# Seven block products for gate and val, one PSUM bank for attention

## The chip, the cores and the metric

The kernel runs on one core of a Trainium2 chip. Its time is the device time in microseconds of one execution; the time before is 975.1 us, the median of three runs (974.89 to 975.76). The engines are TensorE (PE, matmuls; its weight loads are listed as PEld), VectorE (DVE), ScalarE (ACT), GpSimd (POOL) and SyncE (SP), which here issues all DMAs, transposing ones too. Every engine works through its own instructions in order; semaphores tie them together.

## The reference

Attention over keys and values that are averaged in groups of eight, then a gated feed-forward layer over all 4608 tokens:

```python
# q, k, v: (8, 8, 576, 64); pool = 8, Sp = 72
k_p = k.reshape(B, H, Sp, pool, D).mean(axis=3)
v_p = v.reshape(B, H, Sp, pool, D).mean(axis=3)
scores = scale * np.matmul(q, k_p.transpose(0, 1, 3, 2))
scores = scores - np.max(scores, axis=-1, keepdims=True)
attn = np.exp(scores)
attn = attn / (np.sum(attn, axis=-1, keepdims=True) + 1e-09)
out = np.matmul(attn, v_p)
...
x = np.ascontiguousarray(attn_out.transpose(0, 2, 1, 3)).reshape(B * S, H * D)
...
g = x @ w_gate                       # (4608, 512) @ (512, 1536)
silu = g * (1.0 / (1.0 + np.exp(-g)))
val = x @ w_val
return (silu * val @ w_out).astype(np.float32)
```

## The kernel before

**Tiles and chunks.** The 4608 tokens go in nine tiles of 512. A tile is worked in twelve chunks of 128 of the 1536 hidden features. `side` makes gate or val of a chunk: x and the weights are kept as a high and a low f16 part, and for each of four blocks of 128 input features it issues three matmuls of 512 token columns (high x high L797, low x high L798, high x low L799), 12 for gate and 12 for val. ACT makes the tanh of gate (L807), DVE `gated` (L810) and `times_val` (L815), which leaves h in val's PSUM bank; ACT copies h to `hh` (fp32r) and `hb` (bf16), and DVE forms the low half `hl` = h - hh (L1080). `project` adds 12 matmuls a chunk (L824, L830, L831) into four accumulator banks, one chunk later than gate and val. `wo_b`, a bf16 copy of w_out, is made by GpSimd in tile 2. After the last chunk `store` copies the accumulators to `ob` and sends them out (L839).

**Banks.** PSUM has eight banks: four accumulators, gv0 and gv1, and two (`ps_att`) in which attention's scores, values and sums take turns.

**Attention.** It goes by pieces of 128 or 64 tokens, five to a tile. `ask` scales and splits the queries (ACT L523 and L524, POOL L525). `front` computes scores of two groups of four heads (PE L542, L543), takes off the maximum (`less_max`, DVE L552 and L553), the exponential (ACT L564), the sums (L571 to L573), splits the weights into `half` (ACT L620 to L625, POOL L630 and L633) and lets SP issue a transposing DMA to `pt` (L637). `back` multiplies by the values (PE L658, L659), divides (DVE L664), makes the high and low part of x (ACT L757, DVE L759) and lets SP transpose them into the tile's x (L764). A tile's gate and val cannot begin before x of all its pieces. `prep` loads and sums k, v and q of the next batch and splits them (POOL L272 to L274, DVE L267, L328, L339 to L360).

**What sets the order.** Tile 0, with the attention of the first two batches, is one hand-written list of jobs (`ORDER`, in `first_tile`). From tile 1 on (`hidden_tiles`), the chunks are the frame, and at four places of each chunk `slot(vector, scalar)` lets the waiting lines of attention go on: back, front, ask and prep are generators that ask for so much DVE and ACT time, and `slot` gives what its room (`ROOM`) allows. If a tile begins and pieces of it are missing, a loop calls `slot` with endless room until they are done. The order on each engine is that in which the program writes its instructions.

## Time and profile before

| | before |
|---|---|
| median of three runs | 975.1 us |
| the profiled execution: span | 973.8 us |
| TensorE busy, granted clock over the span | 97%, 0.993 |
| DVE, ACT, POOL busy | 58%, 47%, 25% |

The span goes from the first to the last instruction of the profiled execution; the runs' times take in what lies around it. Matmul rows overlap one another in the records, so a row's duration is longer than the distance to the next. A row of a group gives the line, engine, operation, what it writes and reads, shapes and count, then busy us and mean ns of one, then the engine's idle time ahead of these instructions and what ended it. A row of what an engine waits for gives us in total, times, and the longest. A row of the timeline gives start and duration in us.

### The profile page before, as it was taken

The numbers are of one execution on the slowest core, as the hardware profiler recorded it, in microseconds if no ns is written. First come the engines' busy times: TensorE is split into PE (matmuls) and PEld (weight loads), VectorE is DVE, ScalarE is ACT, GpSimd is POOL, SyncE is SP. The second block draws the span as 40 slices with busy tenths as digits, with TensorE's granted clock in tenths as the row PEclk, the third lists the DMA queues.
The fourth block names the chain that finished last, engine by engine and source line by source line (L and its number), as shares of the span: only waits on it lengthen the run. The fifth ranks groups of instructions, "written<-read, shape, count | busy, mean of one in ns | idle before, by whom it ended". The sixth has DMA issues, their size and how long they took to land.

```text
span 973.8 us, 14306 instructions
## 1 busy us (share of the span) xinstructions
PE 939.7 (97%) x5486; PEld 498.4 (51%) x5486; DVE 566.0 (58%) x1005; ACT 461.2 (47%) x864; POOL 241.3 (25%) x327
## 2 busy tenths in 40 slices
PE   5779999799999999999999999999999999999998
PEld 4657545354555555554555555554545555444443
DVE  6788877667766675586446675674444454323222
ACT  3898883245554553544254544552454443222222
POOL 4533336035226230521025211620121201000000
PEclk9899999999999999999999999999999999999999
DMA  9855426246437342653047232840231222001001
GB/s 349 237 154 208 154 109 171 80 115 186 92 109 211 102 83 79 187 127 82 13 88 235 57 70 87 251 86 15 77 83 43 71 66 55 11 1 44 0 1 44
DMA packets 155524, 103.02 MB, mean 106 GB/s; under 512 B 113216, under 2 KB 141888, under 8 KB 153920
## 3 DMA queue, kind: packets, MB, share of 16 engines
q1 hardware_dynamic: 155456, 102.11, 37.3%
q8 instruction: 43, 0.70, 0.3%
q14 instruction: 25, 0.20, 0.1%
HBM read 67.63 MB, written 9.44 MB: 79 GB/s over the span
## 4 chain that ended last, share of the span: by engine, by line
PE 87%; DMA 6%; POOL 2%; ACT 2%; issue 1%; DVE 1%; SPq 0%; POOLq 0%; DVEq 0%; ACTq 0%
PE gv L797 18%; PE gv L798 18%; PE gv L799 18%; PE acc L824 10%; PE acc L830 9%; PE acc L831 9%; DMA pt<-half 2%; DMA kr<-k_rows 1%; DMA in<-v_rest 1%; DMA in<-k_rows 1%; PE ps L542 1%; PE ps L658 1%; PE ps L543 1%; PE ps L659 1%; DMA k<-k_rows 1%
## 5 line engine op out<-in xcount | busy, mean ns | idle before, releaser
L797 PE MATMUL gv<-x,wgv_h 128*128 128x512 f16 (+1 forms) x888 | 332.0, 374 | 3.8 <-ACT x L669 1.8
L798 PE MATMUL gv<-x,wgv_h 128*128 128x512 f16 (+1 forms) x888 | 331.8, 374 | 1.3 <-DVE x L673 1.3
L799 PE MATMUL gv<-x,wgv_l 128*128 128x512 f16 (+1 forms) x888 | 331.9, 374 | 0.5 <-DVE wgv_l L253 0.5
L810 DVE SCALAR_TENSOR_TENSOR hf<-hf,gv 128x512 f32<-128x512 f32 (+1 forms) x111 | 74.1, 668 | 171.6 <-ACT hf L807 171.3
L807 ACT ACTIVATE hf<-gv,un 128x512 f32<-128x512 f32 (+1 forms) x111 | 74.8, 674 | 193.9 <-PE gv L799 193.9
L1076 ACT CAST hh<-gv 128x512 fp32r<-128x512 f32 x96 | 56.3, 586 | 227.2 <-DVE gv L815 227.2
L831 PE MATMUL acc<-hb,wo_l 128*128 128x512 bf16 x384 | 145.5, 379 | 0.0
L824 PE MATMUL acc<-hh,wo_h 128*128 128x512 f32 (+1 forms) x444 | 139.5, 436 | 0.0
L799 PEld LDWEIGHTS <-wgv_l 128*128 128x128 f16 x888 | 87.0, 98 | 102.2 <-issue 1.7
L798 PEld LDWEIGHTS <-wgv_h 128*128 128x128 f16 x888 | 87.0, 98 | 98.1 <-issue 4.7
L797 PEld LDWEIGHTS <-wgv_h 128*128 128x128 f16 x888 | 87.4, 98 | 94.3
L1080 DVE TENSOR_TENSOR hl<-gv,hh 128x512 bf16<-128x512 f32 x96 | 66.3, 691 | 111.0 <-ACT hb L1077 111.0
L525 POOL TENSOR_TENSOR box<-qt,box 64x512 f16<-64x512 f32 (+1 forms) x60 | 64.0, 1067 | 227.8 <-issue 160.9
L815 DVE SCALAR_TENSOR_TENSOR gv<-gv,un,hf 128x512 f32<-128x512 f32 (+1 forms) x111 | 82.3, 741 | 63.0 <-PE gv L799 62.3
L830 PE MATMUL acc<-hl,wo_b 128*128 128x512 bf16 x288 | 109.8, 381 | 0.0
L824 PEld LDWEIGHTS acc<-hh,wo_h 128*128 128x128 f32 x444 | 83.2, 191 | 24.2 <-ACT hh L969 0.3
L630 POOL TENSOR_TENSOR half<-sc,half 128x512 f16<-128x512 f32 (+1 forms) x30 | 34.7, 1158 | 215.8 <-ACT half L620 193.6
L831 PEld LDWEIGHTS <-wo_l 128*128 128x128 bf16 x444 | 43.7, 98 | 37.9
L1077 ACT CAST hb<-gv 128x512 bf16<-128x512 f32 x96 | 56.8, 591 | 0.0
L830 PE MATMUL acc<-hl,wo_h 128*128 128x512 bf16 (+1 forms) x156 | 56.7, 368 | 0.0
L830 PEld LDWEIGHTS <-wo_b 128*128 128x128 bf16 x288 | 28.3, 98 | 42.2 <-issue 16.6
L523 ACT ACTIVATE qt<-qt,inv 128x512 f32<-128x512 f32 (+1 forms) x60 | 40.9, 682 | 0.0
(143 smaller groups left out, 1121.5 us busy)
## 6 DMA issues: line engine op xcount, KB each, us to landing
ws<-w_all SPq DMA_DIRECT2D x12, 1536.0 KB, 7.1
qt<-q_twice SPq DMA_DIRECT2D x48, 256.0 KB, 3.2
out_t<-ob SPq DMA_DIRECT2D x36, 256.0 KB, 2.3
in<-k_rows SPq DMA_DIRECT2D x12, 576.0 KB, 3.9
in<-q_rows SPq DMA_DIRECT2D x12, 576.0 KB, 5.2
in<-v_main SPq DMA_DIRECT2D x12, 512.0 KB, 4.3
in<-v_rest SPq DMA_DIRECT2D x12, 512.0 KB, 5.7
qt<-q_rows SPq DMA_DIRECT2D x8, 256.0 KB, 4.3
```

Source lines behind the costliest of these rows:

```text
L525: nc.gpsimd.tensor_sub(o[rows], qt[rows], o[rows])
L797: nc.tensor.matmul(o, wh, x["h"][:, j, a:e], start=(j == 0), stop=False)
L798: nc.tensor.matmul(o, wh, x["l"][:, j, a:e], start=False, stop=False)
L799: nc.tensor.matmul(o, wl, x["h"][:, j, a:e], start=False, stop=(j == NJ - 1))
L807: nc.scalar.activation(hf, gate, AF.Tanh, scale=un[:, c, 0:1])
L810: nc.vector.scalar_tensor_tensor(out=hf, in0=hf, scalar=1.0, in1=gate, op0=ALU.add, op1=ALU.mult)
L815: nc.vector.scalar_tensor_tensor(out=out, in0=val, scalar=un[:, c, 2:3], in1=hf, op0=ALU.mult, op1=ALU.mult)
L824: nc.tensor.matmul(o, wo_h[:, c, js], hh[:, :n], start=begin, stop=False)
L830: nc.tensor.matmul(o, wo[:, c, js], hl[:, :n], start=False, stop=False)
L831: nc.tensor.matmul(o, wo_l[:, c, js], hb[:, :n], start=False, stop=end)
L1077: nc.scalar.copy(hb[:, :n], val)
L1080: nc.vector.tensor_sub(hl[:, :n], val, hh[:, :n].bitcast(F32))
```

## The change

**Seven products.** From tile 2 on, nine of the twelve chunks (0 to 8; chunks 9 to 11 come first in the tile, as before) get gate and val by Strassen's scheme in Winograd's form. The 2 x 2 blocks of the weights are gate and val by the first and second half of the input features; those of x are feature halves by halves of the 512 tokens. Each of seven products is six matmuls of 256 columns (`product`, L997). The sums of products are made in PSUM by accumulation, by two ACT copies of 128x256 (one within a bank, one into the gate bank), an ACT copy to SBUF (`rs`) and two DVE additions of 128x256 (L1284, L1331). A chunk's products 5, 1, 6 and 2 are issued during the chunk ahead of it. Val turns between the banks gv1 and gv2.

**Sums of weights and of x.** In tile 1, `fast_weights` makes for each of the nine chunks the four weight sums: one DVE addition of the high and low parts (L940, into the single buffer `fw`), four on GpSimd (L942 to L945), ACT copies to f16, and three on GpSimd for the low halves (L958). `fast_x` does the like for x at the start of each tile from 2 on (L965, L967 to L970, L975), in two halves. Both are a new line, `extra`, that `slot` serves first.

**Attention.** From chunk 8 of tile 1 on, scores, values and sums share one bank, and the two groups of scores go one after the other. `front` is cut in two (`front`, `soft`), k's and q's sums are made in halves, and the planner keeps a running time of PE, DVE and ACT (`now`) from which the room of each slot is worked out. The numbers `LANDS` and `CLEAR` keep a sum away from its load, and a bank away from its reader.

**The rest.** h is written to SBUF by `times_val`; its low half is made by GpSimd in the nine chunks, by DVE in the others (L1258); `hb` and `wo_b` become strided views of hh and of w_out. k's sums and the values of the first batches share memory with `xc`.

The core of the diff:

```diff
-ROOM = (1200, 1200), (1200, 1500), (1200, 1200), (2400, 1200)
+ROOM = (2500, 2500)
+FAST = 9
+FAST_ROOM = (3400, 2800), (2700, 2100), (1400, 900), (0, 0), (2000, 0), (2000, 1900), (2400, 4200)
+FAST_FIRST, FAST_THEN = 3, 5
+ONE_BANK = (1, 8)
 LEAD = 3
-AHEAD = 3
+LANDS = 3800
+CLEAR = 650
+AHEAD = 9
...
-    ps_att = ctx.enter_context(tc.tile_pool(name="ps_att", bufs=2, space=bass.MemoryType.PSUM))
+    early = ctx.enter_context(tc.tile_pool(name="early", bufs=1))
+    ps_att = ctx.enter_context(tc.tile_pool(name="ps_att", bufs=1, space=bass.MemoryType.PSUM))
...
-        pss = scores(b, s0, m, t["qs"])
...
+        for groups in ((0,), (1,)) if now["one"] else ((0, 1),):
+            pss = scores(b, s0, m, t["qs"], groups=groups)
...
+    def fast_weights(c):
+
+        yield 1400, 0
+        f = xp.tile([P, 2 * DM], F32, name="fw", tag="f", bufs=1)
+        g_h, g_l = (a[:, c].rearrange("p i j f -> p (i j f)") for a in (wgv_h, wgv_l))
+        nc.vector.tensor_add(f, g_h, g_l)
+        a11, a12, a21, a22 = (f[:, i * HT : (i + 1) * HT] for i in range(4))
+        nc.gpsimd.tensor_add(a22, a21, a22)
+        nc.gpsimd.tensor_sub(a21, a11, a21)
+        nc.gpsimd.tensor_sub(a11, a22, a11)
+        nc.gpsimd.tensor_sub(a12, a12, a11)
+        yield from after(3500)
+        yield 0, 1300
...
+        for o, cs in outs[:2]:
+            nc.scalar.copy(o, f[:, cs])
+        for (o, cs), (hi, _) in zip(outs[2:], outs[:2]):
+            for at in range(cs.start, cs.stop, TILE):
...
+                nc.gpsimd.tensor_sub(o[:, w], f[:, at:e], hi[:, w])
...
+    def product(o, k, c, x, xc, begin):
+
+        for j in range(HJ):
...
+            for n, (a, b) in enumerate(((w[0], xh), (w[0], xl), (w[1], xh))):
+                nc.tensor.matmul(
+                    o, a, b, start=begin and j + n == 0, stop=j == HJ - 1 and n == 2,
+                    skip_group_check=True,
+                )
...
+                    def fourth():
+                        slot(*FAST_ROOM[4])
+                        if new:
+                            seed_fast(new)
+                        slot(*FAST_ROOM[5])
+                        product(t["r"], 4, c, x, xc, False)
+                        times_val(hf, hf, t["val"], un, c)
+                        hh = high_of(hf, n)
+                        slot(*FAST_ROOM[6])
+                        pending.append((acc, *ends, i, c, hh, low_of(nc.gpsimd, hf, hh, n)))
```

**A chunk on DVE.** This is DVE's row in a chunk of tile 3 with attention beside it, before: `gated`, attention's low part of x, `times_val` and the low half, then two operations of `prep`.

```order
L810 SCALAR_TENSOR_TENSOR hf<-hf,gv_3321 128x512
L759 SCALAR_TENSOR_TENSOR box<-ps,r,box 128x512
L815 SCALAR_TENSOR_TENSOR gv_3322<-gv_3322,un,hf 128x512
L1080 TENSOR_TENSOR hl<-gv_3322,hh 128x512
L477 TENSOR_TENSOR mx_3197<-mx_3197 128x1
L328 TENSOR_REDUCE mx_3197<-box 128x1 x2
```

The same place of a chunk with seven products, after (`rs` is the kept product, L734 attention's division, L845 its low part of x):

```order
L901 SCALAR_TENSOR_TENSOR hf<-hf,gv_4867 128x512
L1331 TENSOR_TENSOR gv_4822<-gv_4822,rs 128x256
L734 TENSOR_TENSOR ps<-ps,ri 128x512
L907 SCALAR_TENSOR_TENSOR hf<-gv_4822,un,hf 128x512
L845 SCALAR_TENSOR_TENSOR box<-ps,r,box 128x512
L1284 TENSOR_TENSOR gv_4974<-gv_4918,rs 128x256
```

The low half has left DVE and two additions of half the width have come in, one of them for the chunk that follows.

**Tile 1 on GpSimd and DVE.** Before, GpSimd has query splits (L525), batch sums (L272 to L274) and the low half of attention's weights there:

```order
L525 TENSOR_TENSOR box<-qt,box 64x4x128 x4
L272 TENSOR_TENSOR in<-in 128x2x256
L273 TENSOR_TENSOR in<-in 128x2x128
L274 TENSOR_TENSOR box<-in 128x128
L272 TENSOR_TENSOR in<-in 128x2x256
L273 TENSOR_TENSOR in<-in 128x2x128
L274 TENSOR_TENSOR box<-in 128x128
```

After, GpSimd from the last sum of one weight build to the low halves that free its buffer (L587 is the query split, L283 to L285 the batch sums, L671 and L672 the low half of attention's weights):

```order
L945 TENSOR_TENSOR fw<-fw 128x256
L587 TENSOR_TENSOR box<-qt,box 64x4x128
L283 TENSOR_TENSOR in<-in 128x2x256
L284 TENSOR_TENSOR in<-in 128x2x128
L285 TENSOR_TENSOR box<-in 128x128
L283 TENSOR_TENSOR in<-in 128x2x256
L284 TENSOR_TENSOR in<-in 128x2x128
L285 TENSOR_TENSOR box<-in 128x128
L671 TENSOR_TENSOR half_130<-sc,half_130 128x512
L672 TENSOR_TENSOR half_130<-sc,half_130 128x2x32
L958 TENSOR_TENSOR ws_l<-fw,ws_h 128x512
L958 TENSOR_TENSOR ws_l<-fw,ws_h 128x256
```

And DVE in tile 1, after, where L940 fills `fw` for the next build:

```order
L901 SCALAR_TENSOR_TENSOR hf<-hf,gv_2099 128x512
L940 TENSOR_TENSOR fw<-wgv_h,wgv_l 128x1024
L907 SCALAR_TENSOR_TENSOR hf<-gv_2100,un,hf 128x512
L1258 TENSOR_TENSOR hl<-hf,hh 128x512
L614 TENSOR_REDUCE mx<-ps 128x4
L615 TENSOR_TENSOR sc<-ps,mx 128x288
L614 TENSOR_REDUCE mx<-ps 128x4
L615 TENSOR_TENSOR sc<-ps,mx 128x288
```

On GpSimd ten other operations stand inside a build, and on DVE the fill of `fw` stands ahead of `times_val`, the low half and `less_max`.

**The start of tile 3.** SP before, at the last transpose into tile 3's x (`x_2888`), followed by transposes of attention's weights and queries for the pieces behind, and only then tile 2's output:

```order
L764 DMA_TRANSPOSE x_2888<-box_1705 128x8x64
L637 DMA_TRANSPOSE pt_3742<-half0_132 128x16x128
L509 DMA qt_3788<-q_twice 128x4x128
L509 DMA qt_3790<-q_twice 128x4x128
L637 DMA_TRANSPOSE pt_3874<-half1_133 128x16x128
L839 DMA out_t<-ob_3984 128x512 x2
```

SP after, the same place (`x_2986` is tile 3's x, `x_4133` tile 4's):

```order
L850 DMA_TRANSPOSE x_2986<-box_1470 128x8x128
L557 DMA qt_4088<-q_twice 128x4x128
L557 DMA qt_4090<-q_twice 128x4x128
L707 DMA_TRANSPOSE pt_4122<-half0_129 128x16x128
L850 DMA_TRANSPOSE x_2986<-box_1702 128x8x64
L850 DMA_TRANSPOSE x_4133<-box_1470 128x8x128
L1009 DMA out_t<-ob_4238 128x512 x2
```

And DVE after, between the last `times_val` of tile 2 and the first use of tile 3's x (L614 and L615 are `less_max`, L632 to L638 sums of attention):

```order
L907 SCALAR_TENSOR_TENSOR hf<-gv_3904,un,hf 128x512
L845 SCALAR_TENSOR_TENSOR box<-ps,r,box 128x512
L632 TENSOR_REDUCE sm<-sc 64x8
L637 TENSOR_SCALAR sm<-sm 64x8
L638 RECIPROCAL ri<-sm 64x8
L614 TENSOR_REDUCE mx<-ps 128x4
L615 TENSOR_TENSOR sc<-ps,mx 128x288
L614 TENSOR_REDUCE mx<-ps 128x4
L615 TENSOR_TENSOR sc<-ps,mx 128x288
L734 TENSOR_TENSOR ps<-ps,ri 64x512
L632 TENSOR_REDUCE sm<-sc 128x8
```

Two score groups and the values of tile 3's last piece now stand between the two tiles, and the transpose into x_2986 comes right ahead of tile 2's output and behind pt_4122, which belongs to a later piece.

## The prediction

> **What bounds the kernel now.** I read the page's totals and chain first, then the busy time by stretches, then what TensorE (PE) waits for, then single rows.

> ```profile
> PE 939.7 (97%) x5486; PEld 498.4 (51%) x5486; DVE 566.0 (58%) x1005; ACT 461.2 (47%) x864; POOL 241.3 (25%) x327
> ...
> PE 87%; DMA 6%; POOL 2%; ACT 2%; issue 1%; DVE 1%; SPq 0%; POOLq 0%; DVEq 0%; ACTq 0%
> PE gv L797 18%; PE gv L798 18%; PE gv L799 18%; PE acc L824 10%; PE acc L830 9%; PE acc L831 9%; DMA pt<-half 2%; DMA kr<-k_rows 1%; DMA in<-v_rest 1%; DMA in<-k_rows 1%; PE ps L542 1%; PE ps L658 1%; PE ps L543 1%; PE ps L659 1%; DMA k<-k_rows 1%
> ```

> The chain of waits is PE for 87%, and 54% of it is the three gate/val lines. The stretches (busy us of PE, PEld, DVE, ACT, POOL, then granted clock, DMA share, GB/s) say where that holds:

> ```profile
> 150.00:240.00 90.00, 83.82 (x499) 43.50 (x496) 61.88 (x103) 35.61 (x68) 32.58 (x41) 1.00 0.52 145
> 600.00:690.00 90.00, 90.00 (x513) 45.74 (x512) 53.89 (x98) 38.90 (x78) 22.89 (x30) 1.00 0.42 113
> 780.00:870.00 90.00, 90.00 (x484) 45.07 (x482) 35.42 (x58) 29.98 (x57) 5.45 (x8) 1.00 0.14 36
> ```

> In the tiles that the change rewrites, PE is never idle, while DVE has 36 us of 90 free beside full attention, ACT 51 and POOL 67. So PE time that goes comes off the end, until something else is late. All that PE waits for is short:

> ```profile
> PE ps L536 <- DVE ksum L267: 8.5, 2, 6.9
> PE ps L646 <- DMA pt<-half: 4.1, 3, 2.7
> PE ps L381 <- DMA vr<-v_main: 2.5, 2, 1.4
> PE ps L181 <- DVE sc L553: 2.4, 1, 2.4
> ```

> **What PE gains.** PE rows overlap, so the price of a matmul is the distance of starts. First the gate and val sides of a chunk in the last tile, with the matmul ahead of them (start, duration), then a 256-column side in tile 0, and the group of weight loads (busy time, mean ns):

> ```profile
> 856.47 0.38 PE L831 MATMUL acc<-hb,wo_l 128*128 128x512 bf16 x1
> 856.69 0.38 PE L797 MATMUL gv<-x,wgv_h 128*128 128x512 f16 x1
> ...
> 861.65 0.38 PE L799 MATMUL gv<-x,wgv_l 128*128 128x512 f16 x1
> ```

> ```profile
> 85.99 0.28 PE L797 MATMUL gv<-x,wgv_h 128*128 128x256 f16 x1
> ...
> 87.20 0.27 PE L799 MATMUL gv<-x,wgv_l 128*128 128x256 f16 x1
> ...
> L797 PEld LDWEIGHTS <-wgv_h 128*128 128x128 f16 x888 | 87.4, 98 | 94.3
> ```

> 24 matmuls (gate 12, val 12) start within 4.96 us: 4.96 / 23 = 0.2157 us each. Twelve of 256 columns start within 1.21 us: 1.21 / 11 = 0.110, which I carry as 0.109, as half the columns would have it. So half the columns cost half the time although each loads its own weights; the loads' 98 ns stay below it. A projection matmul takes 0.22 (856.47 to 856.69), and a chunk 5.18 + 12 x 0.22 = 7.8. A changed chunk issues 7 products x 6 = 42 x 0.109 = 4.58 us for 24 x 0.2157 = 5.18: 0.595 less. Nine chunks in seven tiles are 63: **37.5 us off PE**. Projection keeps its twelve matmuls. Replacing the copy of w_out by a strided view costs nothing: both forms stand in before.

> ```profile
> L830 PE MATMUL acc<-hl,wo_b 128*128 128x512 bf16 x288 | 109.8, 381 | 0.0
> L830 PE MATMUL acc<-hl,wo_h 128*128 128x512 bf16 x132 | 50.3, 381 | 0.0
> ```

> **What is added on the other engines.** A changed chunk adds two DVE sums of 128x256 and two ACT copies of 128x256 (estimates of 0.43 and 0.4, from the 128x288 row L553 below and half of L620), drops ACT's hb cast, and sends DVE's low half to GpSimd. Prices (busy time, mean ns | idle before):

> ```profile
> L630 POOL TENSOR_TENSOR half<-sc,half 128x512 f16<-128x512 f32 x24 | 27.8, 1159 | 160.1 <-ACT half L620 138.0 <-DVE sm L571 11.9 <-ACT half L621 10.3
> L272 POOL TENSOR_TENSOR in<-in 128x512 f32<-128x512 f32 x24 | 30.6, 1273 | 14.4 <-DMA in<-v_main 7.9 <-issue 2.2 <-DVE sm L571 2.0
> L273 POOL TENSOR_TENSOR in<-in 128x256 f32<-128x256 f32 x24 | 17.8, 743 | 1.9
> L274 POOL TENSOR_TENSOR box<-in 128x128 f32<-128x128 f32 x24 | 11.3, 470 | 1.9
> L525 POOL TENSOR_TENSOR box<-qt,box 64x512 f16<-64x512 f32 x48 | 55.8, 1163 | 174.8 <-issue 114.2 <-PE ps L543 30.3 <-ACT box L524 28.4
> L1080 DVE TENSOR_TENSOR hl<-gv,hh 128x512 bf16<-128x512 f32 x96 | 66.3, 691 | 111.0 <-ACT hb L1077 111.0
> ```

> The low half takes 1.16 there for 0.69. It is wanted by the fifth matmul of the chunk's projection, behind 3 us of other products, so in steady chunks PE covers it. Walked through one chunk by these prices, each DVE or ACT result that the seven products need is ready 0.8 to 3 us of PE work ahead; I take nothing there, with 0 to 3 us over all for the range. If that cover were gone, 0.5 us a chunk would be 31 us, most of the gain. The x sums at each start of a tile take two halves of a DVE sum (1.38), four 128x256 on GpSimd (3.0), an ACT cast (1.2) and two 128x512 on GpSimd (2.3): 16 us, and up to 23 with attention's work between, in the 21.7 us that three normal chunks leave. That is 0 to 1.5 us a tile; I take 2 in sum. The tail has the last low half on GpSimd, 0.5 longer; with its hand-over I take 1.

> **Tile 1.** Nine weight builds stand in it. One issues on GpSimd four 128x256 (4 x 0.743), one 128x512 (1.16) and two 128x256 of low halves: 5.6 us, nine 50.5. Beside them stand four batch sums (1.273 + 0.743 + 0.470 = 2.49 each, 9.9), nine query splits (1.163, 10.5) and the low halves of attention (6.6): 78 us in the 86 that eleven chunks of 7.8 us leave. There is one `fw` buffer, so L940 of the next build waits on DVE for GpSimd's last L958, with times_val (L907), the low half (L1258) and less_max (L614, L615) queued behind it, and PE behind those. If GpSimd never starves, PE loses 2.4 to 4 us; walking the order by these durations I get 5.1 and 2.5 us before two value groups and 6.3 and 2.3 before two score groups, 16 together. Builds can slide against the waits of others, which the walk doesn't let them; I take 7, nearer the low end, and keep both ends.

> **Starts of tiles.** A tile's first matmul needs x of all its pieces. At tile 3's start the order puts two score groups on the one bank and then the values of the last piece with no chunk between, and SP has the transpose of another piece's weights ahead of x's. Prices of that chain:

> ```profile
> L552 DVE TENSOR_REDUCE mx<-ps 128x4 f32<-128x288 f32 x64 | 28.8, 450 | 4.7 <-PE ps L536 2.5 <-PE ps L543 2.1
> L553 DVE TENSOR_TENSOR sc<-ps,mx 128x288 f32<-128x288 f32 x64 | 29.3, 458 | 4.0
> L564 ACT ACTIVATE sc<-sc,logunit,p2s 128x576 f32<-128x576 f32 x24 | 21.0, 876 | 8.1 <-DVE sc L553 8.1
> L620 ACT CAST half<-sc 128x512 f16<-128x512 f32 x24 | 14.7, 612 | 0.2
> L664 DVE TENSOR_TENSOR ps<-ps,ri 128x512 f32<-128x512 f32 x24 | 16.6, 690 | 0.0
> L757 ACT ACTIVATE box<-ps,r 128x512 f16<-128x512 f32 x24 | 16.7, 694 | 18.5 <-DVE ps L664 17.1 <-issue 1.4
> L759 DVE SCALAR_TENSOR_TENSOR box<-ps,r,box 128x512 f16<-128x512 f32 x24 | 17.8, 743 | 0.8 <-ACT box L757 0.8
> ```

> ```profile
> pt<-half SPq DMA_TRANSPOSE x40, 3.7
> x<-box SPq DMA_TRANSPOSE x30, 2.8
> L637 SPq DMA_TRANSPOSE pt<-half x40: 1225/1592/3304, 26.9 to 823.3; - x40
> ```

> There the chain is 2 x (0.3 scores + 0.91 max and difference) = 2.4, exp 0.88, casts 2.1 (L620 and the smaller ones), the rest of the weights' low half on GpSimd 0.5, issue of pt 1.6, landing of x 2.8: 10.3 us, in which PE has little to do: 10. At tile 2's start PE has 2.6 us of projection after the last val side; behind that side stand on DVE L907 (0.76), the cast (0.6), L1258 (0.69) and L845 (0.74), then x's landing (2.8): 5.6 us, so 3 stay open, and up to 6 with pt's issue in front. I take 5. At tile 5's start L845 stands behind the last L907: 0.76 + 0.74 + 2.8 = 4.3 with 1.3 of PE work: 3. The other tiles have x earlier. Sum **18**; if pt's transpose is through early 10, with every chain 2 us longer 24.

> **One bank.** From tile 1's chunk 8 the two score groups go one after the other, which is in these walks; 2.4 us of old waiting at one bank (L181 above) go.

> **The sum** against the profiled 973.8: -37.5, +7 (tile 1), +18 (starts), +2 (x sums), +1 (tail), -2.4 = 961.9. The median of the three runs, 975.1, stands 1.3 over the span: **963 us**.

> **A clock.** In 40 to 80 us, where PE was idle for 8.8 of 40 us, the granted clock fell to 0.87:

> ```profile
> 40.00:80.00 40.00, 31.18 (x241) 23.99 (x241) 30.68 (x58) 35.34 (x56) 13.17 (x18) 0.87 0.68 184
> ```

> So three long stalls may cost a microsecond or two each besides; 0 to 5 is in the range and not in the sum. [...]

> **Rivals.** *A, all is covered.* Builds slide, starts lose 3 to 6 us only: 973.8 - 37.5 + 3 + 5 + 1 + 1.3 = 946 to 950. For it: DVE, ACT and POOL have room in every stretch. Against: the order at tile 3's start has no PE work to cover the chain.

> *B, DVE and GpSimd block one another in tile 1, and it ends slower.* Rows of before show an operation standing while the other engine has one under way:

> ```profile
> 102.20 1.85 DVE L210 TENSOR_SCALAR ws<-ws 128x1536 uint16<-128x1536 uint16 x1
> 102.43 2.54 POOL L587 TENSOR_TENSOR sc<-sc,ri 128x576 f32<-128x576 f32 x1 [3.36 <-DVE ri L583]
> ...
> 120.68 1.15 POOL L587 TENSOR_TENSOR sc<-sc,ri 128x576 f32<-128x576 f32 x1 [3.33 <-DVE ri L583]
> L253 DVE SCALAR_TENSOR_TENSOR wgv_l<-wf,sw,wgv_h x24: 732/746/1757, 47.8 to 154.5; 128x512 f16<-128x512 f32 x24
> ```

> L587 took 2.54 beside L210 and 1.15 alone. L940 reads two SBUF tensors (estimate 2 x 0.69 = 1.38), and the low half of normal chunks now reads SBUF twice as well. Nine and twelve of them are 12.4 + 8.3 = 20.7 us in which GpSimd would stand; its 78 become 99 in 86, 13 over, and with the walk's 16 tile 1 costs up to 29: 963 - 7 + 16 to 29 = 972 to 985. It decides from 17 us in tile 1. [...]

> *C, the seven products cost more than 0.109 each*, by alternating x and sums or because weight loads of 98 ns leave 11 ns only: at 0.112, 63 x 42 x 0.003 = 8 us more, 971. Against it: the 256-column side is exactly such a row of loads.

> *D, the steady chunks are not covered*: 31 us as above, 994. Against it: the free time of DVE and ACT in those stretches.

> **How the numbers follow.** Forecast, by the bounds of tile 1 and the starts 951 to 972, 0.50; A 0.18; B 0.20; C 0.08; D 0.04. The range takes most of A and nearly all of B: **944 to 984**. About 0.2% (2 us) is what a measurement tells from no change. Faster than 973 are the forecast, A and most of C, 0.73; within 0.2% the upper edges of the forecast and C and the lower of B, 0.05; slower the rest of B, and D, 0.22.

> **What would show it.** 256-column rows 0.109 apart in tiles 2 to 8 with no idle of PE inside them prove the gain. The waits of PE should name L940 or L907 or less_max in 130 to 215 (7 us; over 16 is B, with L942 to L958 longer than 0.75 and 1.2), and x's transposes at the starts of tiles 2, 3 and 5 (5, 10, 3). The forecast is wrong if PE waits inside steady chunks, or if the starts show no idle.

## The result and the profile after

| | before | after |
|---|---|---|
| median | 975.4 us (4 runs) | 1029.0 us (4 runs, 1023.2 to 1033.3) |
| ratio after / before | | 1.054 [1.049, 1.058] |
| profiled span | 973.8 us | 1030.5 us |
| mean granted clock of TensorE | 0.993 | 0.967 |

The change makes the kernel 5.4% slower; the prediction was 963 us, 944 to 984. From the page of after, the totals, the granted clock in tenths over 40 slices, and the chain by engine:

```profile
PE 929.0 (90%) x6521; PEld 610.2 (59%) x6620; DVE 616.6 (60%) x1115; ACT 502.2 (49%) x989; POOL 444.8 (43%) x525
...
PEclk9889999988989999799999899999999999999999
...
PE 60%; DVE 14%; POOL 10%; DMA 6%; issue 5%; ACT 5%; SPq 1%; POOLq 0%; DVEq 0%; ACTq 0%
```

PE's share of the chain fell from 87% to 60%; DVE and POOL together went from 3% to 24%. PE's busy time fell by only 10.7 us, since rows at a lower clock are longer (after 200 us L883's of 512 columns take 0.63 us at clock 0.50 and 0.38 at 1.00, medians; e5 below, the same matmuls at a clock of 1.00 from 188 to 969 us, has 911.3). GpSimd is 43% busy over the span, yet its part of the chain went from 2% to 10%: an average does not show where it is full. The stretches of tiles 1 to 4 and of tile 7 do (columns as in the prediction); below them stand tiles 1 and 2 of before:

```profile
188.00:318.00 130.00, 109.29 (x581) 53.63 (x591) 76.24 (x124) 53.54 (x107) 86.64 (x105) 0.91 0.35 87
318.00:434.00 116.00, 100.98 (x747) 68.16 (x758) 78.73 (x151) 54.95 (x114) 51.89 (x61) 0.93 0.39 102
434.00:542.00 108.00, 97.20 (x748) 66.20 (x759) 67.86 (x125) 54.51 (x121) 52.37 (x61) 0.98 0.44 112
542.00:655.00 113.00, 100.05 (x735) 67.16 (x744) 69.32 (x130) 53.67 (x115) 53.09 (x61) 0.97 0.40 102
...
854.00:946.00 92.00, 90.50 (x627) 61.86 (x636) 35.01 (x61) 31.04 (x64) 22.32 (x23) 1.00 0.15 27
...
```

```profile
188.00:290.00 102.00, 101.02 (x601) 51.83 (x598) 70.82 (x135) 51.41 (x105) 31.96 (x40) 1.00 0.44 117
290.00:390.00 100.00, 100.00 (x610) 51.25 (x609) 63.93 (x114) 48.22 (x99) 35.18 (x51) 1.00 0.45 119
```

In these two tiles of before PE idled 1.0 us; in the four of after it idles 20.7, 15.0, 10.8 and 13.0, at a granted clock of 0.91 to 0.98. Tile 7, with attention only up to 871 us, is hardly ever idle. What PE waits for, after (the largest first, without one row of tile 0):

```profile
PE ps L604 <- DVE box L845: 11.6, 11, 3.1
PE ps L728 <- DMA pt<-half: 8.8, 2, 6.5
...
PE ps L604 <- DVE sc L615: 7.6, 8, 2.0
PE ps L728 <- DVE box L845: 6.5, 5, 2.2
PE ps L604 <- POOL box L587: 6.2, 3, 4.1
PE ps L604 <- DVE x L743: 5.7, 1, 5.7
```

All are attention's score and value groups (L604, L728). Those for L845 and L615 are at the bank, which DVE has yet to read; the others are for GpSimd's split of the queries, for a transfer, and in tile 1, where attention still had two banks, for L743. The products' own waits (L997) stand further down, 7.3 us together.

**Theories.** *S*: the sums cost the time, as *W* those of the weights, as *X* those of x. As *G* they do it by GpSimd's time, as *Q* because what follows in DVE's and ACT's queues stands behind them; as *F* the fill of the single buffer `fw` (L940) is what holds DVE. *B*: the one bank costs it. *P*: the planner's new order costs it. *L*: the seven products themselves do not gain.

### The profile page after: what moved, and what is told of

It is laid out like the page before. It is cut to its first block, busy times and chain, and to the rows that moved or that the text cites. A ratio compares the mean times of both kernels' runs of the same rounds, so it can differ in the third digit from the quotient of the medians.

```text
span 1030.5 us, 16984 instructions
## 1 busy us (share of the span) xinstructions
PE 929.0 (90%) x6521; PEld 610.2 (59%) x6620; DVE 616.6 (60%) x1115; ACT 502.2 (49%) x989; POOL 444.8 (43%) x525
## 3 DMA queue, kind: packets, MB, share of 16 engines
q1 hardware_dynamic: 155456, 102.11, 37.5%
## 4 chain that ended last, share of the span: by engine, by line
PE 60%; DVE 14%; POOL 10%; DMA 6%; issue 5%; ACT 5%; SPq 1%; POOLq 0%; DVEq 0%; ACTq 0%
PE gv L997 24%; PE acc L919 18%; PE gv L883 5%; PE gv L884 4%; PE gv L885 4%; DMA pt<-half 2%; DVE hf L907 2%; POOL box L587 2%; DMA in<-q_rows 1%; POOL xc L975 1%; DVE hf L901 1%; PE ps L398 1%; DVE fx L965 1%; PE ps L604 1%; POOL ws_l L958 1%
## 5 line engine op out<-in xcount | busy, mean ns | idle before, releaser
L1258 POOL TENSOR_TENSOR hl<-hf,hh 128x512 bf16<-128x512 f32 x63 | 81.5, 1293 | 195.4 <-ACT hh L1252 193.3
L919 PE MATMUL acc<-hl,wo_h 128*128 128x512 bf16 (+1 forms) x413 | 154.8, 377 | 4.6 <-POOL hl L1258 0.2
L883 PE MATMUL gv<-x,wgv_h 128*128 128x512 f16 (+1 forms) x384 | 145.5, 379 | 11.2 <-DMA x<-box 4.2
L884 PE MATMUL gv<-x,wgv_h 128*128 128x512 f16 (+1 forms) x384 | 145.2, 378 | 1.3 <-DVE x L743 1.3
L885 PE MATMUL gv<-x,wgv_l 128*128 128x512 f16 (+1 forms) x384 | 145.3, 378 | 0.8 <-DVE wgv_l L264 0.8
L919 PE MATMUL acc<-hh,wo_l 128*128 128x512 bf16 (+1 forms) x376 | 143.7, 385 | 2.4 <-issue 0.6
L587 POOL TENSOR_TENSOR box<-qt,box 64x512 f16<-64x512 f32 (+1 forms) x60 | 66.5, 1109 | 140.8 <-ACT box L586 113.6
L997 PEld LDWEIGHTS <-wgv_h 128*128 128x128 f16 x1008 | 98.3, 98 | 42.2 <-issue 6.3
L907 DVE SCALAR_TENSOR_TENSOR hf<-gv,un,hf 128x512 f32<-128x512 f32 x96 | 71.8, 748 | 59.8 <-PE gv L997 37.9
L997 PE MATMUL gv<-xc,wgv_h 128*128 128x256 f16 x504 | 90.0, 274 | 5.1 <-DVE gv L1331 4.1
L997 PE MATMUL gv<-xc,ws_h 128*128 128x256 f16 x504 | 89.9, 274 | 2.6 <-ACT gv L1278 2.6
L997 PE MATMUL gv<-x,wgv_h 128*128 128x256 f16 x504 | 91.3, 277 | 0.0
L997 PEld LDWEIGHTS <-ws_h 128*128 128x128 f16 x756 | 73.0, 98 | 27.6 <-issue 4.2
L1284 DVE TENSOR_TENSOR gv<-gv,rs 128x256 f32<-128x256 f32 x63 | 27.2, 432 | 72.0 <-PE gv L997 60.4
L997 PE MATMUL gv<-x,wgv_l 128*128 128x256 f16 x252 | 69.7, 276 | 0.0
L997 PE MATMUL gv<-xc,ws_l 128*128 128x256 f16 x252 | 69.1, 274 | 0.0
```

The source lines that it names most:

```text
L587: nc.gpsimd.tensor_sub(o[rows], qt[rows], o[rows])
L883: nc.tensor.matmul(o, wh, x["h"][:, j, a:e], start=(j == 0), stop=False)
L884: nc.tensor.matmul(o, wh, x["l"][:, j, a:e], start=False, stop=False)
L885: nc.tensor.matmul(o, wl, x["h"][:, j, a:e], start=False, stop=(j == NJ - 1))
L907: nc.vector.scalar_tensor_tensor(out=out, in0=val, scalar=un[:, c, 2:3], in1=hf, op0=ALU.mult, op1=ALU.mult)
L919: nc.tensor.matmul(acc[j][:, a:e], w[:, c, j * P : (j + 1) * P], h[:, :n], start=begin and at < NJ, stop=end and w is wo_l,)
```

## The experiments

Every time is a median of 4 to 12 runs beside runs of before on the same chip. For most kernels I also read the length of each tile, from the first projection matmul of a tile to that of the next (of tile 8 to that of its last chunk):

| us, tile | 1 | 2 | 3 | 4 | 5 | 6 | 7 | 8 |
|---|---|---|---|---|---|---|---|---|
| before | 101.5 | 100.8 | 99.3 | 100.6 | 98.5 | 100.1 | 96.2 | 81.2 |
| after | 131.3 | 116.1 | 107.8 | 113.1 | 98.5 | 100.0 | 91.6 | 77.1 |
| e1, no products, no sums | 105.8 | 105.9 | 104.2 | 108.3 | 104.1 | 106.2 | 97.0 | 81.5 |
| e2, as e1 with two banks | 102.9 | 104.1 | 103.7 | 100.5 | 99.0 | 100.6 | 96.2 | 81.5 |
| e5, products, no sums | 105.8 | 99.6 | 101.3 | 103.2 | 100.5 | 100.8 | 92.8 | 77.1 |
| e4, no builds | 106.9 | 102.2 | 108.9 | 107.0 | 109.6 | 100.0 | 91.8 | 77.1 |
| e6, no x sums | 131.1 | 109.9 | 102.3 | 102.9 | 100.8 | 100.8 | 92.7 | 77.1 |
| e20, sums without GpSimd | 111.2 | 110.0 | 101.7 | 108.3 | 98.0 | 99.4 | 91.7 | 77.0 |
| e9, later fill of fw | 114.9 | 143.3 | 102.5 | 111.8 | 98.9 | 100.0 | 91.7 | 77.1 |

Tile 1 of after, which has the builds, is 30 us longer than before; tiles 7 and 8 together are 8.7 us shorter, and tiles 5 and 6 the same.

### Taking the change apart

**e1_no_products**: no chunk by seven products, no sums; planner, one bank and hh view stay.

```diff
-FAST = 9
+FAST = 0
```

> The seven products and all their sums are gone (twelve normal chunks in every tile); the one attention bank from tile 1's chunk 8, the halved score groups and the new planner stay. PE's work is that of before. If the sums of weights and x on GpSimd and DVE made the loss (theory S), the waits go with them: 973 to 980, and no half clock after 100 us. If the one bank made it (theory B), the waits of the scores and values for L845 and L615 (27 us in the changed kernel) stay, with some of the half clock: 995 to 1015.

Measured 1009.6 against 976.7, ratio 1.034 [1.032, 1.035]. A good half of the loss is there without one product or sum. The waits of PE in e1:

```profile
PE ps L604 <- DVE sc L615: 10.6, 13, 1.2
...
PE ps L728 <- DVE box L845: 7.9, 10, 1.3
```

23 short stalls, 18.5 us: a score group waits until `less_max` has read the group ahead of it out of the bank, a value group behind the same DVE queue.

**e2_no_products_two_banks**: the same with attention on two banks.

```diff
-ONE_BANK = (1, 8)
+ONE_BANK = (99, 0)
```

> As the run without products, and attention keeps two banks to the end (val stays in one bank); both score groups go together again. Only the new planner, the low half of h from SBUF and the strided views are left of the change. S and B: 970 to 978. If the planner's own order is bad (theory P: attention too late), 985 or more, and PE waits for x at the starts of tiles.

Measured 984.3, 1.008 [1.007, 1.010]. So the one bank costs 25 us (1009.6 - 984.3) and what is left of the change 8 (984.3 - 976.7).

**e5_no_sums**: products stay, neither sums of weights nor of x; the products read unsummed parts.

```diff
-                join("extra", fast_x(x, xc))
...
-                        join("extra", fast_weights(c))
```

> The whole change, but no sums of weights and of x are made; the products take parts of the weights and of x themselves (same matmuls, wrong output). One bank stays. S: tile 1 falls back by 20 to 25 us, the starts of tiles by 2 to 5 us each: 960 to 985. B: only tile 1's 17 us of builds and some x sums go, the waits for the bank stay in tiles 2 to 4: 1000 to 1010.

Measured 977.8, 1.001 [0.999, 1.003], as S has it. Against e1 the seven products take off 32 us; L falls. What the products gain pays for the one bank and the planner's order and nothing more, and adding the sums costs all the rest, 51 us (1029.0 - 977.8).

**e3_two_banks**: products and sums stay, attention gets its second bank from an accumulator (the fourth block of the projection is added to the third).

```diff
+                if (i, c) == ONE_BANK:
+                    free_banks[:] = [(ps_att, "att"), (ps_acc, "acc3")]
```

> The whole change, but attention has two banks: the fourth output block of the projection is added into the third's accumulators from tile 1 on (same matmuls, the output of these two blocks is wrong), and its bank goes to attention. B: the waits for L845 and L615 fall from 27 to under 8 us and half of the half clock in tiles 2 to 4 goes: 985 to 1000. S: little of it, 1012 to 1030, with tile 1 still 20 us longer than before.

Measured 1036.3, 1.062 [1.059, 1.065]: slower than after, where B had to gain. Waits of PE in e3:

```profile
PE ps L604 <- DVE box L845: 18.0, 8, 5.5
...
PE gv L998 <- POOL xc L976: 11.2, 2, 8.7
...
PE gv L998 <- ACT xc L974: 6.4, 2, 4.3
```

The waits at the bank did not go, and waits of the first products for the x sums (L974, L976, the casts and low halves of xc) came beside them. So the bank's 25 us are its price where no sums stand beside it; with the sums a second bank alone gives nothing back. With it the score groups also go together again and the planner no longer keeps `CLEAR`; why it is worse stays open.

**e4_no_weight_sums** and **e6_no_x_sums**: one of the two sums left out, and the products that would read them read unsummed parts.

```diff
-                    if i == 1 and c < FAST:
-                        join("extra", fast_weights(c))
```

> The whole change without the weight builds of tile 1 (products 3, 6 and 7 take unsummed weights, wrong output); x sums stay. Without both it was 977.8, with both 1029.0. If the builds carry the loss, also that of tiles 2 to 4 by what they push behind (theory W): 980 to 990, tile 1 under 108 us. If the x sums at the tile starts carry that of tiles 2 to 4 (theory X): 1000 to 1010, only tile 1 shorter.

```diff
-                join("extra", fast_x(x, xc))
```

> The whole change without the sums of x (products take x itself, wrong output), with the weight builds. The x sums cost 20 us where no builds stood. If the two add up: 1006 to 1012. If x sums only cost because attention is behind by then: under 1000 or over 1015.

Measured 998.3, 1.022 [1.018, 1.025], and 1014.4, 1.039 [1.037, 1.041]. The builds cost 31 us beside x sums (1029.0 - 998.3) and 37 without (1014.4 - 977.8), the x sums 15 and 20. Tile 1 alone falls from 131.3 to 106.9 without builds. Neither run lies in a range expected: e4 is between W and X, and e6 2 us above what adding up would give.

**e20_sums_without_gpsimd**: DVE's and ACT's part of both sums stays, GpSimd's operations in them go.

```diff
-        nc.gpsimd.tensor_add(a22, a21, a22)
...
-            nc.gpsimd.tensor_sub(b11, b12, b11)
```

> The whole change, with the sums' DVE additions and ACT casts, but without their GpSimd operations (the four sums and the low halves of weights and of x; wrong output). Without any sums it was 977.8, with all 1029.0. If GpSimd's time is what the sums cost (theory G): 978 to 990. If it is the DVE and ACT work standing in their queues (theory Q): 1000 to 1025.

Measured 994.6, 1.019 [1.017, 1.020]. It lies between G and Q. Of the sums' 51 us, 34 go with GpSimd's part (1029.0 - 994.6) and 17 stay with the rest, so G takes some two thirds and Q one third; but what DVE and ACT lose by waiting for GpSimd's results goes here with G.

**e7_low_half_dve**: the low half of h goes back from GpSimd to DVE in the 63 chunks.

```diff
-                        pending.append((acc, *ends, i, c, hh, low_of(nc.gpsimd, hf, hh, n)))
+                        pending.append((acc, *ends, i, c, hh, low_of(nc.vector, hf, hh, n)))
```

> The whole change, but the low half of h stays on DVE in the nine chunks too. In tiles 2 to 8 GpSimd loses 63 x 1.29 us of work and DVE gains 63 x 0.69. If GpSimd's load in steady tiles is a part of the loss (theory G): 1010 to 1020. If DVE, which reads the one bank, is what is short there (theory B): 1030 to 1045. Tile 1 stays at 131 us in both.

Measured 1094.8, 1.122 [1.118, 1.126]. Sixty-three operations of 0.69 us (43 us, L1080 of before) on an engine that is 60% busy cost 66 us, far beyond both expectations; the planner's rooms were left as they are. Waits of PE in e7:

```profile
PE ps L604 <- DVE sc L615: 20.6, 15, 5.1
PE ps L728 <- DVE box L845: 15.7, 6, 5.1
PE gv L883 <- DMA x<-box: 15.4, 5, 4.1
```

The same waits as in after, the first two 2.4 to 2.7 times as long: DVE's queue sets when the bank comes free and when x is there. That part of the change helps.

### Giving the waits room

**e8_no_products_clear**: e1, with the planner keeping 2000 ns between a bank and its reader.

```diff
-CLEAR = 650
+CLEAR = 2000
```

> The run without products on one bank, with CLEAR 2000 for 650: the planner leaves 2 us of PE work for 0.65 between a reader of the bank and the next writer. If the one bank costs because the next score or value group comes before DVE has read the bank (theory B): the 22 us of waits for L615 and L845 fall under 6, 984 to 992. If it costs because attention as a whole gets too late or by PE work in between: 1005 or more.

Measured 991.3, 1.015 [1.012, 1.018]: 18 us less than e1, and the waits for L615 and L845 are gone from the top. In their place, in e8:

```profile
PE ps L728 <- DMA pt<-half: 9.4, 4, 3.4
```

So most of B's price without sums is the planner's distance, not the bank as such; some of it turns into later attention weights. The whole change with this distance alone was not run.

**e9_late_fill**: a build waits 3.5 us more before it is done, so that the next L940 finds `fw` free.

```diff
+        yield from after(3500)
```

> The whole change, but the next weight build is asked for only 3.5 us of PE work after the last low half of the one ahead. If tile 1 is long because L940 stands on DVE waiting for the single buffer (12 us of DVE idle there, with times_val and less_max behind it; theory F): these waits go, tile 1 falls by 10 to 15 us, 1010 to 1020, also if two builds slip into tile 2. If GpSimd's work itself is what attention waits for (theory G): tile 1 falls by under 6 us and what is gained comes back in tile 2, 1022 to 1035.

Measured 1035.2, 1.059 [1.056, 1.062]. Tile 1 falls by 16 us, and DVE's waits at L940 from 12.4 to 0.6, as F has it; tile 2 rises by 27, with the last two of the nine builds now in front of its x sums in the same line. The first wait of PE in e9:

```profile
PE gv L998 <- ACT xc L974: 25.7, 2, 19.6
```

So the wait for the single buffer was a cause of tile 1's length, but not of the whole loss: the amount of work stays, and two builds moved into tile 2 cost more there than the wait did.

**e10_spread_clear**: three chunks by products in tile 2, six in tile 3, nine from tile 4; builds in tiles 1 to 3; CLEAR 2000.

```diff
+FAST_IN = {1: 0, 2: 3, 3: 6}
```

> Correct variant: builds spread over tiles 1 to 3 (three each; tile 2 has three chunks with products, tile 3 six, from tile 4 nine), and CLEAR 2000. Nine of the 63 chunks lose 0.56 us each, 5 us. If W and B hold, both costs shrink: 955 to 975. If not, 990 or more.

Measured 999.5, 1.023 [1.019, 1.026]. It is the second branch expected. Tiles 1 to 4 are 39 us longer than before, tiles 5 to 8 together 13 shorter.

**e11_two_banks_wait**: e2 with later use of what attention makes.

```diff
-LEAD = 3
+LEAD = 4
...
-WAIT = 3
+WAIT = 5
```

> The run without products on two banks, with WAIT 5 for 3 and LEAD 4 for 3: a piece's values come two slots later. If the 8 us that this planner costs over before are values ahead of their transposed weights (PE waits for pt 4 us), 974 to 979; if they are attention's order as such, 982 to 988.

Measured 986.1, 1.009 [1.007, 1.012]; no gain over e2's 984.3. Greater distances do not bring back the 8 us, of which some 4 are the strided view's (below).

**e12_late_products**: on e11, products only in five chunks of tile 7 and nine of tile 8, builds in tiles 6 and 7, one bank only from the end of tile 7.

```diff
+FAST_IN = {**{i: 0 for i in range(1, 7)}, 7: 5}
...
+ONE_BANK = (7, 11)
```

> Correct variant: two banks and normal chunks up to tile 7's seventh chunk; weight builds in tiles 6 (five) and 7 (four); products in five chunks of tile 7 and nine of tile 8, where attention has ended or nearly; one bank from there; WAIT 5, LEAD 4. 14 x 0.56 = 7.8 us off the run with WAIT 5 alone. If products are worth their PE time where attention's bank and GpSimd aren't needed: 966 to 972. If builds cost as in tile 1 even there: 980 or more.

Measured 989.6, 1.013 [1.011, 1.015]. Against e11 tiles 7 and 8 are 2.4 and 4.4 shorter, as the price of a product says; tile 6, with five builds beside attention, is 8 longer. So beside attention a build costs about 1.6 us of PE, and a chunk by products gains 0.5 a tile.

### A version on the kernel before

**e15_before_last_tile**, **e16_last_tile_hb** and **e17_last_tile_gpsimd** take the kernel of before, with its order and its banks, and work only the last tile by seven products; the sums stand where attention is over, in the end of tile 7 and the first chunks of tile 8.

```diff
+            end_tile = i == len(tiles) - 1
+            order = [*range(FAST, NCH), *range(FAST)] if end_tile else list(range(NCH))
...
+                if over() and i >= len(tiles) - 2:
+                    if end_tile and step < HJ:
+                        fast_x(x, xc, step)
```

e15 has eight such chunks, weight sums on DVE, and the strided view of hh in place of hb in every chunk.

> Correct variant of the kernel before: its planner and two banks are kept, and products are used in eight chunks of the last tile alone, where no attention is left. The eight weight builds (sums on DVE, low halves on GpSimd) stand one to a chunk behind attention's last step, the second PSUM bank for val is one that attention no longer needs. 8 x 0.56 = 4.5 us less PE work, 0.5 of it lost at the end: 970 to 973. If builds delay PE even without attention: 976 or more.

Measured 982.7, 1.006 [1.004, 1.009]. The tiles without products are 0.3 to 0.4 us longer each than before (tiles 3 and 7: 1.5), and in tile 8 the store's copies stand behind the builds on DVE. e16 has hb back in the normal chunks.

> As the run before (products in eight chunks of the last tile of the old kernel), mended in two places: normal chunks have their bf16 copy of h again (matmuls that read the strided upper half of hh lie 0.226 us apart, those with the copy 0.216), and builds stand behind the output copies of tile 7, not ahead of them. If these two were its loss: 970 to 974, tile 8 under 78 us from its first to its last projection against 81.2. If not: 977 or more.

Measured 983.4, 1.007 [1.004, 1.009]. Tiles 1 to 7 are those of before within 0.3 us; tile 8 takes 87.2, with this wait in it, of PE for `gated`:

```profile
897.40 0.59 PE L798 MATMUL gv<-x,wgv_h 128*128 128x512 f16 x1 [4.10 <-DVE hf L811]
```

`gated` waits for its tanh on ACT (L808, 895.95), and that stands in ACT's order behind two casts (L877, L861), of which the first waited for x sums on GpSimd until 893.70 and the second for weight sums on DVE.

In e17 seven chunks go by products, the sums are on GpSimd in a buffer of their own, and the casts and low halves come one chunk after the sums.

> Products in seven chunks of the last tile of the old kernel, mended again: the sums of a build stand on GpSimd, with only the first addition on DVE, in a buffer of their own, and the casts and low halves one chunk later, so that neither DVE nor ACT waits for a sum. In the run before this tile lost 7.5 us of idle to builds in DVE's queue. If products pay 0.56 each where nothing waits for their sums: tile 8 77.5 to 79 us from first to last projection (81.2 before), 972 to 974. If not: 976 or more.

Measured 974.3 (12 runs) against 977.4 (17 runs), 0.997 [0.996, 0.999]: 0.3% below the kernel before. Tile 8 takes 78.1 for 81.2, and from 870 us on PE waits only 0.6 us:

```profile
PE acc L825 <- ACT hh L1202: 0.4, 1, 0.4
PE acc L833 <- POOL hl L1203: 0.2, 1, 0.2
```

So the product scheme pays where GpSimd and DVE are free and every sum is a chunk ahead of its user. Which of the things changed since e16 did it, no run separates.

## Why the prediction was wrong

Taken in the order e2, e1, e5, after, the runs give four prices: planner and view +8, one bank +25, products -32, sums +51. That they add up to the 52 us lost is no proof, since each is a difference to the run ahead; and each holds in this order alone (by e3 a second bank gives nothing back once the sums are there). Of the 56.7 us by which the span grew, by its own steps:

| step | forecast | measured |
|---|---|---|
| matmuls of gate and val | -37.5 | -37.5 |
| strided view of hh | 0 | +4 |
| tile 1 | +7 (2.4 to 16) | 16.5 idle and about 10 of clock |
| starts of tiles 2, 3, 5 | 5, 10, 3 | 4.2, 10.1, 2.1 |
| x sums and steady chunks, tiles 2 to 8 | +2 | 37 more idle than before |
| clock in tiles 2 to 4 | 0 | about 10 |
| not placed | | about 1 |

The third row is the 20.7 idle of tile 1's stretch less the 4.2 of tile 2's start in it; the fifth is the 71 idle of all eight stretches up to the last matmul, less 16.5 and 16.4, less 1.5 of before.

**The gain of PE was right.** In tile 8 the projections of two chunks by products start 7.30 us apart:

```profile
990.90 1.17 PE L919 MATMUL acc<-hh,wo_h 128*128 128x512 f32 x4
...
998.20 1.17 PE L919 MATMUL acc<-hh,wo_h 128*128 128x512 f32 x4
```

Before it is 7.85 there, so 0.55 to 0.56 a chunk where 0.595 was forecast. The 0.04 between is not the products' but the view's: the step "costs nothing: both forms stand in before" looked at w_out alone, not at hh, whose upper half is now every second bf16. First after, then before, with hb:

```profile
939.68 0.39 PE L919 MATMUL acc<-hh,wo_l 128*128 128x512 bf16 x1
939.90 0.38 PE L919 MATMUL acc<-hl,wo_h 128*128 128x512 bf16 x1
940.12 0.39 PE L919 MATMUL acc<-hh,wo_l 128*128 128x512 bf16 x1
```

```profile
878.73 0.38 PE L831 MATMUL acc<-hb,wo_l 128*128 128x512 bf16 x1
878.94 0.38 PE L830 MATMUL acc<-hl,wo_b 128*128 128x512 bf16 x1
```

From a matmul with the view to the next it is 0.22 here and 0.226 over many, with hb 0.21 and 0.216: four times a chunk that is 0.04 us, 4 us in the 96 chunks of tiles 1 to 8. The price stood in before already: its tile 0 reads hh by the view, and there these matmuls lie 0.225 apart (median of 35). e15 with the view and e16 without it show the same (0.4 a tile). The 256-column matmuls lie 0.109 apart in tiles 5 to 8, as forecast, so rival C's 0.112 is out.

**The starts were right**: in tile 3's, PE waits 0.4, 2.0, 1.1 and 6.5 us in the order that the prediction walked, 10.1 for its 10. Rows of after:

```profile
408.42 0.21 PE L604 MATMUL ps<-box 128*128 128x72 f16 x1 [2.04 <-DVE sc L615]
409.99 0.23 PE L728 MATMUL ps<-box,pt 128*64 128x64 f16 x1 [1.14 <-DVE sc L615]
...
417.55 0.24 PE L728 MATMUL ps<-box,pt 128*128 128x64 f16 x1 [6.53 <-DMA pt<-half]
```

The last wait was ended by the weights of a later piece, whose values stand in PE's order ahead of tile 3's first matmul; x, with which the walk ended, landed about 0.6 us later (L965, which needs it, starts at 418.20).

**"Which is in these walks", said of the one bank, and "I take nothing there", of the steady chunks, failed.** Of attention, only tile 1 and three starts were walked. One steady chunk was walked for what the products need, and that held (7.3 us of waits at L997); attention's groups in it were left to free shares ("DVE has 36 us of 90 free"), although every score and value group there now has to be read by DVE before the next begins. e1 shows that wait 23 times with no sum on any engine, and without sums the bank costs 25 us where the sum had 0. Rival D, at 0.04, came nearest to the largest row (31 us for 37), but by late results of the products. The planner's new order had no term at all; e2 puts it at some 4 us, the view left out.

**The x sums, "0 to 1.5 us a tile; I take 2 in sum", cost 15 to 20.** That term weighed their length against the chunks they have, not the queue: L965 stands in DVE's order and holds all behind it. Group of after:

```profile
L965 DVE TENSOR_TENSOR fx<-x 128x1024 f32<-128x1024 f16 x14 | 17.1, 1222 | 18.0 <-DMA x<-box 9.5 <-POOL xc L975 8.5
```

DVE stands idle for 18 us ahead of these fourteen, for x's landing and for GpSimd's last low half of the half ahead (one buffer again).

**Tile 1, "I take 7, nearer the low end", took 26.** GpSimd is busy 86.6 of 130 us there, where 78 were counted. Inside the build listed ahead stand nine other operations, not ten. Here four sums of a build stand between two query splits, so the scores that need the second come 4 us late; and DVE stands at L940, behind which `times_val` and the low part of x of an early piece (L743) come late. Rows of after, of GpSimd, PE and DVE in order of time:

```profile
204.32 2.20 POOL L587 TENSOR_TENSOR box<-qt,box 64x512 f16<-64x512 f32 x1
...
210.41 1.15 POOL L587 TENSOR_TENSOR box<-qt,box 64x512 f16<-64x512 f32 x1
```

```profile
211.61 0.21 PE L604 MATMUL ps<-box 128*128 128x72 f16 x1 [4.08 <-POOL box L587]
...
239.03 0.24 PE L604 MATMUL ps<-box 128*128 128x72 f16 x1 [5.72 <-DVE x L743]
```

```profile
234.93 1.23 DVE L940 TENSOR_TENSOR fw<-wgv_h,wgv_l 128x1024 f32<-128x1024 f16 x1 [4.47 <-POOL wgv_l L958]
...
238.24 0.74 DVE L743 SCALAR_TENSOR_TENSOR x<-ps,r,x 128x512 f16<-128x512 f32 x1
```

The upper end of the walk, 16, is the idle time measured; taking less, because "builds can slide", was wrong, and e9 shows where they slide to: into the x sums of tile 2. The sum agrees better than its parts, which is in part luck: the score groups' 6.3 and 2.3 measure 4.1 and 5.7, the value groups' 5.1 and 2.5 measure 1.9 and 2.2, and the 4.1 is for the query split on GpSimd, not for DVE. By e4 builds account for 24 of the 30 us by which the tile grew, tile 2's start and the clock included; the rest is there without them.

**Rival B had the place and part of the mechanism.** Summing how much longer than the median of its form each row of tile 1 is, GpSimd, which B had standing for 20.7 us, loses 6.0 and DVE some 7; in tiles 2 to 8 DVE loses some 24 against 11 before. Such rows, after:

```profile
262.51 2.40 POOL L587 TENSOR_TENSOR box<-qt,box 64x512 f16<-64x512 f32 x2
264.09 1.97 DVE L637 TENSOR_SCALAR sm<-sm 128x8 f32<-128x8 f32 x1
264.87 1.16 POOL L700 TENSOR_TENSOR half<-sc,half 128x512 f16<-128x512 f32 x1
```

L637 works on eight columns, with a median of 0.22 us over its group; here it took 1.97, begun beside a query split and ended within 0.03 us of the L700 behind it. Rows like L637 are in kind what B had; that GpSimd would stand for the whole 20.7 us was the author's estimate from the one row of L587 beside L210, and no run shows it. B left out the one bank and the x sums, which is why its 985 fell short too. How the sums' cost divides between this and plain queueing no run separates.

**The clock, "0 to 5 is in the range and not in the sum", failed.** Stretches of after around tile 3's start, the clock third from the end:

```profile
405.50:410.00 4.50, 0.93 (x18) 0.66 (x18) 3.68 (x8) 2.99 (x6) 3.56 (x3) 0.98 0.43 94
410.00:423.50 13.50, 6.97 (x44) 3.53 (x45) 5.34 (x15) 2.95 (x8) 4.46 (x7) 0.50 0.43 87
423.50:433.00 9.50, 9.32 (x56) 4.58 (x56) 6.73 (x11) 6.90 (x11) 2.92 (x3) 1.00 0.56 120
```

After 4.5 us with 0.9 of work the clock is 0.50 for 13.5 us, 7 of them with matmuls. After 200 us there are ten such stretches, 51 us long, in which PE lost some 20 by the distances of its matmuls. The stretches are 3.41 us long or whole multiples of it, and the 3.41 us ahead of each were not wholly idle (last section); matmuls of L883 to L885 with 512 columns start 0.427 us apart in them, against 0.216 at full clock (medians). The prediction counted three long stalls, by an estimate from the one row of 40 to 80 us; shorter ones did it too, as the 1.90 us that end at 225.00, half a microsecond ahead of a half-clock stretch. e1 has no stall over 1.3 us after 200 us and keeps 0.993 over its span.

## What to carry to other kernels

Here PE was 97% busy, and the edit that shortened its work made the other engines' queues the bound. In such a case price each added operation on DVE or GpSimd by what stands behind it in program order, in every stretch that has a handshake, and not by the engine's free share. A resource that is halved (a bank, a buffer) must be walked in the steady chunk, not only at the joints. If the helper work can stand where its engines are free and a chunk ahead of its use, as in e17, the gain comes out; find that place first.

## What the runs showed of the hardware

Two things were not expected. In these runs a matmul of 512 columns whose moving operand is every second bf16 took about 5% longer: 0.226 against 0.216 us from one start to the next (medians; e15 with the view, e16 without).
